# Transposes on TensorE that take two neighbouring bf16 values as one 32-bit word, in a fused convolution and gated-MLP kernel

## The chip, the cores and the metric

The kernel runs on one core of one Trainium2 chip. The metric is the device time of one execution in microseconds (us). The program is one instruction stream per engine: PE (TensorE, matmuls and transposes; PEld is its weight load), DVE (VectorE), ACT (ScalarE), POOL (GpSimd) and SP (which only issues DMAs here). Each engine works its stream in order, and semaphores hold it where it needs another engine's result.

## The reference, cut to what matters

The kernel computes a forward pass and all its gradients. With S = 2048 rows, D = 1024 and F = 3584:

```python
xn = layernorm(x)                       # S x D
g, u = xn @ w_gate, xn @ w_up           # S x F each
h = g * u
bm = h @ w_down                         # S x D
y = causal convolution of kv with the filter ssm_k, along S, by FFT   # per column
kv = shift_filter(k, shift_k) * v       # 4 taps
out = x + (xn * (y + kv * ssm_D)) * silu(bm)
grads of out for x, k, v, shift_k, ssm_k, ssm_D, w_gate, w_up, w_down
```

All inputs and outputs are bf16; the gradient of w_down needs h by rows, and the forward product needs h turned. A matmul contracts over the 128 partitions, so a matrix that lies by rows has to be turned before its columns can be contracted.

## The kernel before

The work is in stages, one after the other on PE, with other engines' work laid beside it.

**Stage 1, 0 to 52 us.** `layer_norm` (L554) normalizes 16 blocks of 128 rows in chunks of 1, 1, 2, 4, 4 and 4 blocks; most of this is DVE. The result of each block (128 rows by 1024 columns) is turned by eight PE transposes of 128x128 (L596 for the first two blocks, L607 and, for the last two chunks, L619 in `turn_late`) into a PSUM tile `tr`, and copied from there into `XNT` (one tile for four blocks, `[128, 8, 512]`: partition p, group dc, row s holds column dc*128+p). ACT copies even blocks (L609, L621), DVE odd ones (L611, L623): seven copies on DVE in all.

**Stage 2, up to 520 us.** `gu_unit` (L645) works on one slab of 256 columns of w_up and w_gate (14 slabs) and 4 blocks of rows at a time. For each block, 8 matmuls with 512 columns (L661; up and gate lie side by side) go into `psg`, which ACT copies to `gut` (L663). One unit later `multiply` (L672) lets DVE multiply the two halves into `hN` (L213, the line of the helper `tt`), POOL stores hN to DRAM as `Hd`, and a few groups later `turn` (L685) transposes hN on PE (L690, 8 for a unit of 4 blocks), ACT copies the PSUM tile to `hT` (L691), and SP stores that to DRAM as `HTd`, by rows of F. Weight slabs are loaded one slab ahead (`load_slab`, L536).

Beside it runs the forward convolution (`conv_forward`, L701): eight sub-steps `ds`, each an FFT of a piece of kv and one of filter rows, their product, and an inverse FFT. The large butterflies of the FFT are DVE operations at L213 and L283; the small DFTs are PE matmuls against tables (L235), which ACT copies to `SP` (L257, L295; two buffers) for DVE's `W<-SP`. `h_rows` (L738) turns filter rows with PE transposes (L747, L749: 8 for each half, of columns that lie 8 apart) and ACT scales them into `hx` (L750).

What sets the order: the convolution is a generator that `make_pump` (L465) advances. Each of its steps yields an estimate of its DVE time; after each group of 8 matmuls `tick` (L932) advances it until the estimates reach a share of their total that follows the number of groups done. `net` (L244) takes 0.95 of the PE time that the step has entered in `pe_us` off the estimate; `h_rows` enters 0.47 us (L744). A framework then orders each engine's instructions and places the semaphores; the convolution's DVE operations are kept in program order.

**Stage 3, 520 to 719 us.** bm = h @ w_down from HTd (L985), and the gate with its gradients on DVE (`gate`, L1203), which turns the last blocks of `dbm` with eight transposes each (L1238).

**Stages 4 to 6, to the end.** The gradients of w_gate and w_up (L1339, L1356), of w_down (L1434, whose stationary operand is h from `Hd`, loaded by `load_h`, L1371) and of x (L1486), with the backward convolution on DVE beside them.

A transpose is `nc.tensor.transpose(out, in_, ident)`: in_ is loaded as weights, and an identity matrix is the moving operand. `keep_busy` (L519) multiplies the identity with itself 58 and 10 times at the start, to no other end than a busy PE.

Of the kernel before, what the change touches and what calls it, by code (L numbers as in the profile page):

```python
# [19 lines left out]
def build_kernel(  # L20
# [87 lines left out]
    KFd = dram.tile([8, P, 16, 256], BF16, name="KFd")  # L108
    DYFd = dram.tile([8, P, 16, 256], BF16, name="DYFd")
    GUd = dram.tile([NSL, 2, P, 2, 8, SLW], BF16, name="GUd")  # L110
    Hd = dram.tile([NSL, P, 2, NB, P], BF16, name="Hd")
    HTd = [[dram.tile([n, S // 2], BF16, name=f"HTd{i}{n}") for n in (24 * P, 4 * P)] for i in range(2)]
    DGd = dram.tile([NSL, 2, S, SLW], BF16, name="DGd")


    const = ctx.enter_context(tc.tile_pool(name="const", bufs=1))
    ident = const.tile([P, P], BF16, name="ident")
    make_identity(nc, ident[:])
    mhpi = const.tile([P, 1], F32, name="mhpi")
    nc.vector.memset(mhpi[:], -np.pi / 2)  # L120
    negpi = const.tile([P, 1], F32, name="negpi")
# [64 lines left out]
    def turn_tables(psp):  # L186

        for j in range(2):
            for rq in range(2):
                ps = psp.tile([P, 4, 2, P], BF16, name="psY")  # L190
                for i in range(4):
                    for k in range(2):
                        nc.tensor.transpose(ps[:, i, k, :], T4[j][:, 4 * rq + i, k, :], ident[:])
                nc.scalar.copy(out=TI[:, j, 4 * rq:4 * rq + 4], in_=ps[:])
                yield


    def pr(t, i, j):
        if j > i:
            return t[:, i:j + 1:j - i, :]  # L200
        return t[:, i:(j - 1 if j > 0 else None):j - i, :]

    PIN = [False]

# [7 lines left out]
    def tt(o, a, b, op):  # L212
        pinned(V.tensor_tensor(o, a, b, op))  # L213
# [304 lines left out]

    def keep_busy(n):  # L519
        for i in range(n):  # L520
            mm = nc.tensor.matmul(busy[:, i % 4, :], ident[:], ident[:], start=True, stop=True)
        return mm

    keep_busy(58)
# [11 lines left out]
    def load_slab(sl, eng):  # L536
        w = fw.tile([P, DC, 2, SLW], BF16, name="wslab")
        fs = slice(sl * SLW, (sl + 1) * SLW)
        for a, wsrc in ((0, B_w_up), (1, B_w_gate)):
            last = eng.dma_start(out=w[:, :, a, :], in_=wsrc[:, fs].rearrange("(dc p) f -> p dc f", p=P))  # L540
        return w, last

    def ln_load(b0, n, x4):
# [6 lines left out]

    tr_ln, act_copy = [None], [None]
    turn_rows = []

    def layer_norm(b0, n, x4):  # L554
        def small(name, dt=F32):
# [27 lines left out]
        for i in range(n):  # L583
            b = b0 + i
            q, qi = divmod(b, 4)
            if n == 4 and i < 2:
                nc.scalar.activation(x4[:, i, :], x4[:, i, :], ACT.Identity, bias=mean_f[:, i:i + 1])
            else:
                V.tensor_scalar(x4[:, i, :], x4[:, i, :], mean_f[:, i:i + 1], None, op0=ADD)
            last = V.tensor_scalar(x4[:, i, :], x4[:, i, :], RSTD[:, b:b + 1], None, op0=MUL)  # L590
            if b < 2:
                for hh in range(2):
                    ps = ps_st.tile([P, 4, P], BF16, name="tr")
                    for dc in range(4):
                        d0 = (4 * hh + dc) * P
                        tr_ln[0] = nc.tensor.transpose(ps[:, dc, :], x4[:, i, d0:d0 + P], ident[:])  # L596
                    act_copy[0] = nc.scalar.copy(out=XNT[0][:, 4 * hh:4 * hh + 4, b * P:b * P + P], in_=ps[:])  # L597
                if b == 0:
                    with tc.issue_after(tr_ln[0].ins):
                        keep_busy(10)  # L600
                continue
            if b0 >= 8:
                turn_rows.append((x4[:, i, :], q, qi))
                continue
            ps = ps_st.tile([P, DC, P], BF16, name="tr")
            for dc in range(DC):
                tr_ln[0] = nc.tensor.transpose(ps[:, dc, :], x4[:, i, dc * P:(dc + 1) * P], ident[:])  # L607
            if i % 2 == 0:
                act_copy[0] = nc.scalar.copy(out=XNT[q][:, :, qi * P:(qi + 1) * P], in_=ps[:])  # L609
            else:  # L610
                V.tensor_copy(XNT[q][:, :, qi * P:(qi + 1) * P], ps[:])  # L611
        c, r0 = divmod(b0, 8)
        return last, root, st(xnn[:, c, r0:r0 + n, :], x4[:, 0:n, :])

    def turn_late():
        for i, (x, q, qi) in enumerate(turn_rows):
            ps = ps_st.tile([P, DC, P], BF16, name="tr")
            for dc in range(DC):
                tr_ln[0] = nc.tensor.transpose(ps[:, dc, :], x[:, dc * P:(dc + 1) * P], ident[:])  # L619
            if i % 2 == 0:  # L620
                act_copy[0] = nc.scalar.copy(out=XNT[q][:, :, qi * P:(qi + 1) * P], in_=ps[:])  # L621
            else:
                V.tensor_copy(XNT[q][:, :, qi * P:(qi + 1) * P], ps[:])  # L623
        turn_rows.clear()

    nop = lambda: None
# [18 lines left out]
    def gu_unit(sl, b0, n, w, tick):  # L645

        if n == 4:
            turn_of[0] += 1
            if turn_of[0] % 3 == 0 and sl < NSL - 2:
                gut = U[5][:, 2048:4096].rearrange("p (a i f) -> p a i f", a=2, i=4)  # L650
            else:
                gut = fg.tile([P, 2, 4, SLW], BF16, name="gut")
            hN = fg.tile([P, 2, 4, P], BF16, name="hN", bufs=3)
        else:
            gut = lnp.tile([P, 2, 2, SLW], BF16, name="gut_s", bufs=6)
            hN = lnp.tile([P, 2, 2, P], BF16, name="hN_s", bufs=6)
        for i in range(n):
            q, qi = divmod(b0 + i, 4)
            ps = ps_gu.tile([P, 512], F32, name="psg")
            for dc in range(DC):  # L660
                gu_mm[0] = nc.tensor.matmul(ps[:], XNT[q][:, dc, qi * P:(qi + 1) * P],  # L661
                                            w[:, dc].rearrange("p a f -> p (a f)"), start=(dc == 0), stop=(dc == DC - 1))
            nc.scalar.copy(out=gut[:, :, i], in_=ps[:].rearrange("p (a f) -> p a f", a=2))  # L663
            flush(5)
            if i == 0:
                turn_late()
            hn[0]()
            hn[0] = nop
            tick()
        sta(GUd[sl, b0 // 8][:, :, b0 % 8:b0 % 8 + n], gut[:, :, 0:n])  # L670

        def multiply():  # L672
            with tc.issue_after(last.ins) if b0 + n <= 4 and chunk[0] <= 2 else nullcontext():
                by_half = lambda t: t.rearrange("p i (a f) -> p a i f", a=2)
                tt(hN[:, :, 0:n], by_half(gut[:, 0, 0:n]), by_half(gut[:, 1, 0:n]), MUL)
            st(Hd[sl][:, :, b0:b0 + n, :], hN[:, :, 0:n])
            defer(turn)
        hn[0] = multiply

        def store(hT):  # L680
            fr, so = sl % 12 * SLW, b0 % 8 * P
            ld(HTd[b0 // 8][sl // 12][fr:fr + SLW, so:so + n * P].rearrange("(a f) s -> f a s", f=P),
               hT[:, :, 0:n].rearrange("f a i s -> f a (i s)"))

        def turn():  # L685
            hT = fg.tile([P, 2, 4, P], BF16, name="hT") if chunk[0] > 5 else lnp.tile([P, 2, 4, P], BF16, name="hT_s", bufs=5)
            ps = ps_tr.tile([P, 2, 4, P], BF16, name="tr")
            for a in range(2):
                for i in range(n):
                    nc.tensor.transpose(ps[:, a, i, :], hN[:, a, i, :], ident[:])  # L690
            nc.scalar.copy(out=hT[:, :, 0:n], in_=ps[:, :, 0:n])  # L691
            store(hT)

    h_out = []
# [6 lines left out]
    def conv_forward():  # L701
# [36 lines left out]
        def h_rows(ds, c):  # L738
# [2 lines left out]
            hrow = S_["h", ds]  # L741
            if c == 0:
                S_["hx"] = cf.tile([P, NB, P], BF16, name="hx")
            pe_us[0] += 0.47  # L744
            ps = ps_tr.tile([P, 8, P], BF16, name="tr")
            with tc.issue_after(tr_ln[0].ins):
                nc.tensor.transpose(ps[:, 0, :], hrow[:, c, :, 0], ident[:])  # L747
            for r in range(1, 8):
                nc.tensor.transpose(ps[:, r, :], hrow[:, c, :, r], ident[:])  # L749
            nc.scalar.activation(S_["hx"][:, 8 * c:8 * c + 8, :], ps[:], ACT.Copy, scale=WSC)  # L750
            if c == 1:
                h_out.append(ds)
                if ds + 1 < 8:
# [449 lines left out]
    def gate(b, ps):  # L1203
# [31 lines left out]
        def turn():  # L1235
            ps = ps_tr.tile([P, DC, P], BF16, name=tr_name[0])
            for dc in range(DC):
                nc.tensor.transpose(ps[:, dc, :], dbm[:, dc * P:(dc + 1) * P], ident[:])  # L1238
            nc.scalar.copy(out=DBMT[b // 4][:, :, (b % 4) * P:(b % 4 + 1) * P], in_=ps[:])
        if b >= 12:  # L1240
            defer(turn)
# [127 lines left out]
            next(others, None)  # L1369

    def load_h(sl):  # L1371
        h = u8(HSL[sl % 3], "p (a b f) -> p a b f", a=2, b=NB)
        ld(h, Hd[sl])
        hs[sl] = h

    for e in later:
# [172 lines left out]
    for g in range(1, 4):  # L1549
        for b in (4 * g, 4 * g + 2):  # L1550
            end = b == NB - 2
            pss = [ps_x.tile([P, D], F32, name="psx") for i in range(2)]
            for n in range(12 if end else 14):
# [3 lines left out]
                    DBM[n] = u8((7, 0, 1, 9)[n], a=4)  # L1557
                    ld(DBM[n], DBMd[512 * n:512 * n + 512, :].rearrange("(b u) d -> u b d", u=P))
                if end and n == 4:
                    h = u8(2, "p (a b f) -> p a b f", a=2, b=NB)  # L1560
                    ld(h, Hd[NSL - 1])
                if end and n == 8:
                    ln_loads(NB - 1)
                if g < 3:
# [83 lines left out]
```

## Time and profile before

| what | value |
|---|---|
| median of 3 runs | 1929.96 us |
| lowest and highest run | 1929.68, 1931.19 us |
| span of the profiled execution | 1929.5 us |
| PE busy | 1906.4 us (99%), 10843 matmul records |
| DVE busy | 1549.6 us (80%) |
| ACT busy | 638.4 us (33%) |
| POOL busy | 330.5 us (17%) |
| HBM read and written | 194.00 and 185.64 MB |
| transposes of hN, records (L690) | 448, 219 ns each |
| transposes of filter rows (L747, L749) | 128, 218 and 226 ns each |
| ACT copies hT<-tr of 128x1024 (L691) | 52, 1018 ns each |

How to read the page: busy time is a union of the instructions' spans. Matmuls are pipelined: one of 512 columns lasts 379 ns, but in a row they start closer together, so the spacing of starts and not the duration is what a matmul costs in a sequence. A line such as `L690 PE MATMUL tr<-ident,hN` is a group of instructions of one line of the kernel: engine, operation, written tile, read tiles; behind it stand the shape, the number, the busy time and the mean duration, then the idle time of the engine ahead of them and what ended it. L213 is a helper that many parts use, so one goes by the tile's name there. In the waits, `A <- B: t, n, m` says that A waited for B for t us in all, n times, at most m.

### The profile page before, as it was taken

To read this page: it belongs to the slowest core of one execution; us is meant where nothing else is said; L and a number is where in the kernel's file an instruction comes from. 1 tells how busy PE (TensorE), PEld (TensorE's weight loads), DVE (VectorE), ACT (ScalarE), POOL (GpSimd) and SP (SyncE) were. 2 spreads that over 40 slices of the span, in tenths; PEclk is the share of its full clock that TensorE was granted. 3 is DMA by queue.
4 is the path that set the end of the run, shared out by engine and by line. 5 is a ranking of instruction groups with operands and counts; after the bars stand their busy time and mean duration, and the time that the engine had idled before them with its cause. 6 is when DMAs were issued, how large, how long until landed. Compare 5 with 4: busy or idle time off the path is not lost.

```text
span 1929.5 us, 27354 instructions
## 1 busy us (share of the span) xinstructions
PE 1906.4 (99%) x10843; PEld 1031.0 (53%) x10978; DVE 1549.6 (80%) x1730; ACT 638.4 (33%) x942; POOL 330.5 (17%) x461
## 2 busy tenths in 40 slices
PE   8999999999999999999999999999999999999999
PEld 5555555555444456665666666664444444444444
DVE  9999999999937556888899999999996404288884
ACT  5764555555422233343222222222212102011113
POOL 4121212111112210000122131121211101011111
PEclk9999999999999999999999999999999999999999
DMA  8876866758899997666788788575787999889985
GB/s 293 268 259 217 261 209 226 234 196 268 272 270 311 282 313 258 208 202 219 258 246 261 239 248 262 202 272 174 226 253 174 157 205 210 153 170 201 191 177 169
DMA packets 451361, 444.43 MB, mean 230 GB/s; under 512 B 268801, under 2 KB 371613, under 8 KB 436769
## 3 DMA queue, kind: packets, MB, share of 16 engines
q1 hardware_dynamic: 394848, 243.36, 48.0%
q0 software_dynamic: 40064, 169.95, 27.8%
q10 hardware_dynamic: 16320, 29.36, 4.2%
q8 instruction: 86, 1.41, 0.3%
q14 instruction: 43, 0.34, 0.1%
HBM read 194.00 MB, written 185.64 MB: 197 GB/s over the span
## 4 chain that ended last, share of the span: by engine, by line
PE 71%; DVE 18%; DMA 4%; issue 4%; ACT 1%; SPq 1%; POOL 0%; DVEq 0%; ACTq 0%; POOLq 0%
PE psb L1356 20%; PE psb L1339 10%; PE psbm L985 10%; PE psx L1486 10%; PE psb L1434 9%; PE psg L661 6%; DVE W L213 4%; DVE KX L213 2%; DVE HX L213 2%; PE psF L235 2%; DVE dkp L1184 2%; DVE m L213 1%; DVE U L213 1%; DMA dkT<-DKSHd 1%; DVE hN L213 1%
## 5 line engine op out<-in xcount | busy, mean ns | idle before, releaser
L661 PE MATMUL psg<-wslab,U 128*128 128x512 bf16 x1733 | 401.6, 379 | 4.8 <-ACT U L597 1.0
L1356 PE MATMUL psb<-U,U 128*128 128x512 bf16 x1792 | 397.0, 379 | 0.0
L1486 PE MATMUL psx<-U,dgut 128*128 128x512 bf16 x1505 | 331.2, 379 | 2.4 <-DMA dgut<-DGd 0.8
L1486 PEld LDWEIGHTS <-dgut 128*128 128x128 bf16 x1792 | 175.2, 98 | 212.5 <-DMA dgut<-DGd 1.3
L1356 PEld LDWEIGHTS <-U 128*128 128x128 bf16 x1792 | 175.3, 98 | 197.9
L661 PEld LDWEIGHTS <-U 128*128 128x128 bf16 x1792 | 172.5, 98 | 187.3 <-issue 1.8
L1339 PE MATMUL psb<-wdt,U 128*128 128x256 bf16 x1792 | 205.6, 273 | 0.0
L1339 PEld LDWEIGHTS <-U 128*128 128x128 bf16 x1792 | 175.3, 98 | 29.2
L1434 PE MATMUL psb<-U,U 128*128 128x512 bf16 x797 | 175.9, 379 | 0.9
L213 DVE TENSOR_TENSOR W<-W 128x1024 f32<-128x1024 f32 (+1 forms) x174 | 171.6, 1003 | 3.7
L1361 ACT CAST wb<-psb 128x512 bf16<-128x512 f32 x112 | 65.6, 586 | 315.4 <-PE psb L1356 307.3
L985 PE MATMUL psbm<-U,ht 128*128 128x512 bf16 x658 | 144.8, 379 | 0.7
L1434 PEld LDWEIGHTS <-U 128*128 128x128 bf16 x896 | 87.5, 98 | 104.5
L663 ACT CAST gut<-psg 128x512 bf16<-128x512 f32 x156 | 91.6, 588 | 120.8 <-PE psg L661 118.9
L1518 ACT ACTIVATE dx_t<-dxn 128x1024 bf16<-128x1024 f32 x15 | 15.9, 1058 | 325.5 <-DVE dxn L213 325.5
L1184 DVE SCALAR_TENSOR_TENSOR dkp<-dkT,kT 128x1024 bf16<-128x1024 bf16 (+2 forms) x64 | 78.4, 1224 | 39.9 <-DMA dkT<-DKSHd 37.9
L985 PEld LDWEIGHTS <-ht 128*128 128x128 bf16 x672 | 65.7, 98 | 78.6
L213 DVE TENSOR_TENSOR U<-U,dht 128x2048 bf16<-128x2048 bf16 x56 | 68.3, 1221 | 46.4 <-ACT dht L1341 46.4
L1341 ACT CAST dht<-psb 128x512 bf16<-128x512 f32 x112 | 65.7, 587 | 116.3 <-PE psb L1339 116.3
L66 POOL DMA_DIRECT2D Hd<-hN x54 | 37.0, 685 | 292.9 <-DVE hN L213 291.8
L213 DVE TENSOR_TENSOR dxn<-psx,dxna_t 128x1024 f32<-128x1024 f32 x15 | 18.3, 1222 | 79.5 <-PE psx L1486 75.4
L1465 ACT CAST wbs<-psb 128x512 bf16<-128x512 f32 x51 | 29.9, 586 | 145.3 <-PE psb L1434 134.3
(260 smaller groups left out, 2464.6 us busy)
## 6 DMA issues: line engine op xcount, KB each, us to landing
U<-GUd SPq DMA_DIRECT2D x28, 1024.0 KB, 7.7
DGd<-U SPq DMA_DIRECT2D x28, 1024.0 KB, 6.0
GUd<-gut ACTq DMA_DIRECT2D x39, 512.0 KB, 6.0
out_dram<-wb SPq DMA_DIRECT2D x112, 128.0 KB, 3.9
U<-Hd SPq DMA_DIRECT2D x14, 1024.0 KB, 6.0
Hd<-hN POOLq DMA_DIRECT2D x54, 256.0 KB, 4.0
HTd<-hT SPq DMA_DIRECT2D x52, 256.0 KB, 3.9
ht<-HTd SPq DMA_DIRECT2D x6, 1536.0 KB, 11.4
```

The lines of the kernel that those rows point to most:

```text
L213: pinned(V.tensor_tensor(o, a, b, op))
L235: mm = nc.tensor.matmul(ps[:, k].rearrange("p (c d) -> p c d", c=2), T[:, r, k, :], xr[:, r], start=(n == 0), stop=(n == len(rs) - 1 and ( ...
L661: gu_mm[0] = nc.tensor.matmul(ps[:], XNT[q][:, dc, qi * P:(qi + 1) * P], w[:, dc].rearrange("p a f -> p (a f)"), start=(dc == 0), stop=(dc ...
L663: nc.scalar.copy(out=gut[:, :, i], in_=ps[:].rearrange("p (a f) -> p a f", a=2))
L985: mm = nc.tensor.matmul(ps[:, dh * 512:(dh + 1) * 512], ht(fc)[:, i * P:(i + 1) * P], WD[fc // 4][:, fc % 4, dh * 512:(dh + 1) * 512], sta ...
L1184: ins = V.scalar_tensor_tensor(prod[:].rearrange("p r d -> p (r d)")[:, lo:H], dkT[:, 0, lo:H], 1.0, kT[:, 0, 13 + m + lo:13 + m + H], op0 ...
L1339: nc.tensor.matmul(ps[:, x * SLW:(x + 1) * SLW], DBMT[2 * hf + g][:, dc, (b % 4) * P:(b % 4 + 1) * P], wdt[:, dc, :], start=(dc == 0), sto ...
L1341: nc.scalar.copy(out=dht[:, 2 * e:2 * e + 2].rearrange("p b f -> p (b f)"), in_=ps[:])
L1356: nc.tensor.matmul(ps[:], XN[b // 4][:, b % 4, dc * P:(dc + 1) * P], dgus[b // 8][:, :, b % 8], start=(b == 0), stop=(b == NB - 1))
L1361: nc.scalar.copy(out=wb[:, dc % 2].rearrange("p a f -> p (a f)"), in_=ps[:])
L1434: nc.tensor.matmul(ps, h[:, f, b, :], DBM[b // 4][:, b % 4, dh * 512:(dh + 1) * 512], start=(b == 0), stop=(b == NB - 1))
L1486: nc.tensor.matmul(ps[:, dh * 512:(dh + 1) * 512], t[n][:, f, i * P:(i + 1) * P], WGU[n][:, f, dh * 512:(dh + 1) * 512], start=(n == 0 and ...
```

## The change

Two neighbouring bf16 values are read as one 32-bit word, and PE turns words. A 128x128 transpose of words carries 256 columns, so there are half as many: 4 in place of 8. In PSUM, the two halves of a word lie beside each other; the copies out of PSUM read every second bf16 (`halves_of`) and so part the halves again.

A turned word holds two columns 2j and 2j+1 in one partition, so the order of the columns changes, and everything that is contracted with them follows:

- XNT: the words of a row are taken at steps of 4 words, so that partition p holds columns 8p to 8p+7. The weight slabs are loaded in the same order (`(p c) f` in place of `(dc p) f`).
- hN lies as rows of 256 columns in place of two halves of 128; Hd follows, and `load_h` views it so that the matmuls at L1434 find what they found. hT holds columns 2f and 2f+1 in partition f; the store to HTd puts them at rows 2f and 2f+1, so HTd is as it was.
- Filter rows: pairs of residues (2r, 2r+1) are one word; 4 transposes for each half, and `hx` is written as before. The entry in `pe_us` is 0.25.
- The identity is an f32 tile; the transposes that stay bf16 (the tables at L193, dbm at L1238) and `keep_busy` read the upper halves of its words as a bf16 identity with a step of 2.

Matmuls, DMAs and DVE operations stay the same in number, apart from that. The core of the diff:

```diff
-    Hd = dram.tile([NSL, P, 2, NB, P], BF16, name="Hd")
+    Hd = dram.tile([NSL, P, NB, SLW], BF16, name="Hd")
...
-    ident = const.tile([P, P], BF16, name="ident")
-    make_identity(nc, ident[:])
+    ident4 = const.tile([P, P], F32, name="ident4")
+    make_identity(nc, ident4[:])
+    ident = ident4[:].bitcast(BF16)[:, 1::2]
...
+    def turn_pairs(out, in_):
+        return nc.tensor.transpose(out, in_, ident4[:])
+
+    def halves_of(ps):
+        return ps.bitcast(BF16).rearrange("p q (s two) -> p q two s", two=2)
...
-            last = eng.dma_start(out=w[:, :, a, :], in_=wsrc[:, fs].rearrange("(dc p) f -> p dc f", p=P))
+            last = eng.dma_start(out=w[:, :, a, :], in_=wsrc[:, fs].rearrange("(p c) f -> p c f", c=DC))
...
+    def by_pair(t):
+        return t.rearrange("p (q two) s -> p q two s", two=2)
+
+    def in_pairs(x):
+        return x.bitcast(F32).rearrange("p (m q) -> p q m", q=4)
+
+    def turn_row(i, x, q, qi):
+        ps = ps_st.tile([P, 4, P], F32, name="tr")
+        for dc in range(4):
+            tr_ln[0] = turn_pairs(ps[:, dc, :], in_pairs(x)[:, dc])
+        to = by_pair(XNT[q][:, :, qi * P:(qi + 1) * P])
+        if i % 2 == 0:
+            act_copy[0] = nc.scalar.copy(out=to, in_=halves_of(ps[:]))
+        else:
+            V.tensor_copy(to, halves_of(ps[:]))
...
-            hN = fg.tile([P, 2, 4, P], BF16, name="hN", bufs=3)
+            hN = fg.tile([P, 4, SLW], BF16, name="hN", bufs=3)
...
-                by_half = lambda t: t.rearrange("p i (a f) -> p a i f", a=2)
-                tt(hN[:, :, 0:n], by_half(gut[:, 0, 0:n]), by_half(gut[:, 1, 0:n]), MUL)
-            st(Hd[sl][:, :, b0:b0 + n, :], hN[:, :, 0:n])
+                tt(hN[:, 0:n], gut[:, 0, 0:n], gut[:, 1, 0:n], MUL)
+            st(Hd[sl][:, b0:b0 + n, :], hN[:, 0:n])
...
-            ld(HTd[b0 // 8][sl // 12][fr:fr + SLW, so:so + n * P].rearrange("(a f) s -> f a s", f=P),
+            ld(HTd[b0 // 8][sl // 12][fr:fr + SLW, so:so + n * P].rearrange("(f a) s -> f a s", a=2),
...
-            ps = ps_tr.tile([P, 2, 4, P], BF16, name="tr")
-            for a in range(2):
-                for i in range(n):
-                    nc.tensor.transpose(ps[:, a, i, :], hN[:, a, i, :], ident[:])
-            nc.scalar.copy(out=hT[:, :, 0:n], in_=ps[:, :, 0:n])
+            ps = ps_tr.tile([P, 4, P], F32, name="tr")
+            for i in range(n):
+                turn_pairs(ps[:, i, :], hN[:, i, :].bitcast(F32))
+            nc.scalar.copy(out=hT[:, :, 0:n].rearrange("f a i s -> f i a s"), in_=halves_of(ps[:, 0:n]))
...
-            pe_us[0] += 0.47
-            ps = ps_tr.tile([P, 8, P], BF16, name="tr")
+            pe_us[0] += 0.25
+            ps = ps_tr.tile([P, 4, P], F32, name="tr")
+            pairs = hrow.rearrange("p c u r -> p (c u r)").bitcast(F32).rearrange("p (c u r) -> p c u r", c=2, r=4)
             with tc.issue_after(tr_ln[0].ins):
-                nc.tensor.transpose(ps[:, 0, :], hrow[:, c, :, 0], ident[:])
-            for r in range(1, 8):
-                nc.tensor.transpose(ps[:, r, :], hrow[:, c, :, r], ident[:])
-            nc.scalar.activation(S_["hx"][:, 8 * c:8 * c + 8, :], ps[:], ACT.Copy, scale=WSC)
+                turn_pairs(ps[:, 0, :], pairs[:, c, :, 0])
+            for r in range(1, 4):
+                turn_pairs(ps[:, r, :], pairs[:, c, :, r])
+            nc.scalar.activation(by_pair(S_["hx"][:, 8 * c:8 * c + 8, :]), halves_of(ps[:]), ACT.Copy, scale=WSC)
...
-        h = u8(HSL[sl % 3], "p (a b f) -> p a b f", a=2, b=NB)
-        ld(h, Hd[sl])
+        h = u8(HSL[sl % 3], "p (b a f) -> p a b f", a=2, b=NB)
+        ld(U[HSL[sl % 3]][:].rearrange("p (b f) -> p b f", b=NB), Hd[sl])
```

The first two blocks (L596) are turned in the same way, with two PSUM tiles of two words' transposes each; `turn_late` and the body of `layer_norm` call `turn_row`.

More of the change, by code (lines that the diff above doesn't have):

```diff
@@ L192, in turn_tables @@
                     for k in range(2):
-                        nc.tensor.transpose(ps[:, i, k, :], T4[j][:, 4 * rq + i, k, :], ident[:])
+                        nc.tensor.transpose(ps[:, i, k, :], T4[j][:, 4 * rq + i, k, :], ident)
                 nc.scalar.copy(out=TI[:, j, 4 * rq:4 * rq + 4], in_=ps[:])
@@ L520, in keep_busy @@
         for i in range(n):
-            mm = nc.tensor.matmul(busy[:, i % 4, :], ident[:], ident[:], start=True, stop=True)
+            mm = nc.tensor.matmul(busy[:, i % 4, :], ident, ident, start=True, stop=True)
         return mm
@@ L592, in layer_norm @@
                 for hh in range(2):
[L593 to L597, printed above, removed]
+                    ps = ps_st.tile([P, 2, P], F32, name="tr")
+                    for dc in range(2):
+                        tr_ln[0] = turn_pairs(ps[:, dc, :], in_pairs(x4[:, i, :])[:, 2 * hh + dc])
+                    act_copy[0] = nc.scalar.copy(out=by_pair(XNT[0][:, 4 * hh:4 * hh + 4, b * P:b * P + P]), in_=halves_of(ps[:]))
                 if b == 0:
@@ L604, in layer_norm @@
                 continue
[L605 to L611, printed above, removed]
+            turn_row(i, x4[:, i, :], q, qi)
         c, r0 = divmod(b0, 8)
@@ L616, in turn_late @@
         for i, (x, q, qi) in enumerate(turn_rows):
[L617 to L623, printed above, removed]
+            turn_row(i, x, q, qi)
         turn_rows.clear()
@@ L652, in gu_unit @@
                 gut = fg.tile([P, 2, 4, SLW], BF16, name="gut")
-            hN = fg.tile([P, 2, 4, P], BF16, name="hN", bufs=3)
+            hN = fg.tile([P, 4, SLW], BF16, name="hN", bufs=3)
         else:
             gut = lnp.tile([P, 2, 2, SLW], BF16, name="gut_s", bufs=6)
-            hN = lnp.tile([P, 2, 2, P], BF16, name="hN_s", bufs=6)
+            hN = lnp.tile([P, 2, SLW], BF16, name="hN_s", bufs=6)
         for i in range(n):
@@ L1237, in turn @@
             for dc in range(DC):
-                nc.tensor.transpose(ps[:, dc, :], dbm[:, dc * P:(dc + 1) * P], ident[:])
+                nc.tensor.transpose(ps[:, dc, :], dbm[:, dc * P:(dc + 1) * P], ident)
             nc.scalar.copy(out=DBMT[b // 4][:, :, (b % 4) * P:(b % 4 + 1) * P], in_=ps[:])
@@ L1559, in build_kernel @@
                 if end and n == 4:
-                    h = u8(2, "p (a b f) -> p a b f", a=2, b=NB)
-                    ld(h, Hd[NSL - 1])
+                    h = u8(2, "p (b a f) -> p a b f", a=2, b=NB)
+                    ld(U[2][:].rearrange("p (b f) -> p b f", b=NB), Hd[NSL - 1])
                 if end and n == 8:
```

## The prediction

> **What bounds the kernel now.** I read the page's totals and slices first, then the table by stages, the waits, and the timeline where PE last waits for DVE.
>
> ```profile
> PE 1906.4 (99%) x10843; PEld 1031.0 (53%) x10978; DVE 1549.6 (80%) x1730; ACT 638.4 (33%) x942; POOL 330.5 (17%) x461
> ...
> PE   8999999999999999999999999999999999999999
> ...
> DVE  9999999999937556888899999999996404288884
> ```
>
> PE looks like the bound everywhere. But up to slice 11 (530 us) DVE is full as well, and nearly all transposes that change lie there. The stages (columns: stretch, length, then the busy time of each engine):
>
> ```profile
> 10.00:52.00 42.00, 38.39 (x271) 20.63 (x274) 40.20 (x118) 27.00 (x44) 19.35 (x27) 1.00 0.91 303
> 52.00:492.00 440.00, 431.32 (x2666) 243.19 (x2715) 435.42 (x391) 256.88 (x358) 75.47 (x107) 1.00 0.72 238
> 492.00:520.00 28.00, 27.68 (x148) 13.77 (x152) 27.69 (x33) 12.30 (x20) 4.45 (x6) 1.00 0.85 287
> 520.00:560.00 40.00, 39.77 (x210) 20.09 (x212) 12.30 (x11) 9.79 (x12) 1.84 (x2) 1.00 0.80 225
> ```
>
> From 52 to 492 us DVE works 435.4 of 440 us and PE 431.3. DVE has 4.6 us left; it can't follow a PE that is 15 us quicker. Which waits for which shows in the waits of 52 to 530 us and in the timeline at 492 us:
>
> ```profile
> ACT SP L257 <- DVE W L213: 5.3, 5, 1.6
> PE psF L235 <- DVE kv L213: 3.4, 2, 1.9
> ...
> PE tr L690 <- DVE hN L213: 1.7, 1, 1.7
> ```
>
> ```profile
> 491.43 0.68 DVE L213 TENSOR_TENSOR hN<-gut 128x1024 bf16<-128x1024 bf16 x1
> 492.03 1.22 DVE L213 TENSOR_TENSOR W<-SP 128x1024 f32<-128x1024 f32 x1
> 492.16 0.45 PEld L690 LDWEIGHTS <-hN 128*128 128x128 bf16 x8 [2.20 <-DVE hN L213]
> 492.17 0.62 PE L690 MATMUL tr<-ident,hN 128*128 128x128 bf16 x8 [1.71 <-DVE hN L213]
> ```
>
> PE and ACT wait for DVE; no large wait of DVE for PE is listed. The last meeting is at 492.16: PE stands until DVE has multiplied that hN. From there PE's own work runs without a gap to the first L985 at 519.43: in the compiled order 116 matmuls of 512 columns, 24 transposes and 8 matmuls of 256, which at 216, 56 and 109 ns are 27.3 us, and 492.1 + 27.3 = 519.4. (Spacings come from groups of the timeline: ten L661 in 2.32 us with the last 0.379, so 1.94/9 = 216; eight L690 as below; 64 L1339 in 7.15 us, 109.) After 520 us DVE is 30% busy and PE nearly full, so a shift of 519.4 goes straight to the end. **The end is set by: DVE's work ahead of that multiply, plus PE's work behind it.**
>
> **The change part by part.** The rows of today:
>
> ```profile
> 146.01 0.61 PE L690 MATMUL tr<-ident,hN 128*128 128x128 bf16 x8
> ...
> 147.88 0.60 PE L749 MATMUL tr<-ident,U 128*128 128x128 bf16 x7
> ```
>
> ```profile
> L213 DVE TENSOR_TENSOR W<-SP 128x1024 f32<-128x1024 f32 x64 | 74.3, 1220 | 1.3 <-ACT yf L765 0.5
> L623 DVE COPY U<-tr 128x1024 bf16<-128x1024 bf16 x4 | 2.6, 680 | 0.0
> L611 DVE COPY U<-tr 128x1024 bf16<-128x1024 bf16 x3 | 2.0, 675 | 0.0
> ```
>
> *Transposes.* One lasts 219 ns, but in a row they follow every (610-219)/7 = 56 ns, and every (600-226)/6 = 62 where the weights are read at 16-byte steps (L749). Of 704 transposes (448 of h, 128 of normalized rows, 128 of filter rows) 352 remain. Today they are 576 x 56 + 128 x 62 = 40.2 us of PE. The trace has no 32-bit matmul. Bounds of one: 56 ns, as now; 109, as a matmul with as many bytes of moving data (256 columns of bf16); 216, if the array goes through the words four times (as 512 columns); 317, if load (98) and matmul (219) don't overlap. I take 62, since rows and filter words are now read at 16-byte steps like L749, and one instruction still moves 128 columns: PE work falls by 40.2 - 21.8 = 18 us, 15 of it from 52 to 492 us. All of that turns into waiting for DVE. Where does the price matter? From 60 to 520 us PE's nominal work is 451 us, 31 of it transposes (408 of h, 128 of filter rows); 268 remain, and 420 + 268 x price passes the 460 us plus 2 at **about 155 ns**.
>
> [...]
>
> *Copies out of PSUM.* They now read halves of words, 4 bytes apart. On ACT, 1024 f32 (L257, 1019 ns) and 1024 bf16 (L691, 1018 ns) cost the same, so nothing; were they to double, ACT would go from 257 to some 323 of 440 us and still be hidden. On DVE they don't cost the same: the seven copies of L611 and L623 take 680 ns for 1024 bf16, while an f32 read of 1024, also 4 bytes apart, takes 1220. Bounds 0 and 7 x 0.54; I take the upper, the row with the same spacing of data: **+3.7 us**, all between 18 and 52 us, where DVE is full, so paid at 492.
>
> [...]
>
> *The planner.* The filter rows' entry falls from 0.47 to 0.25, so convolution units count as longer and DVE gets them later in the program. Ahead of the multiply that ends at 492.11 the new DVE order has two W<-SP (1.135 us apart) and two KX steps (0.602) fewer: **-3.5 us**. PE's part behind it grows: 123 x 216 + 16 x 109 + 12 x 62 ns = 29.1 against 27.3: **+1.8 us**. The deferred units run after 520 us, where DVE is idle from 531 to 554 and PE's next use of them (L449) is at 542.9, 12 us late enough.
>
> *Layouts.* The hN multiply keeps its 1024 elements (684 ns). Hd's lines double to 2 KB; its stores stay 256 KB each and lie on POOL, busy 75 of 440 us. HTd stores keep their size and place on SP's queue. Weight slabs take rows 8p to 8p+7, still 512-byte pieces; a slab lands in 5.8 and 8.4 us and is wanted some 35 us later, so nothing; only the first has no cover (PE waits 0.6 us for it at 14.5). The f32 identity is made by POOL before the warm-up matmuls (1.4 to 7.5 us), which hide it; the 64 transposes that stay bf16 read it at 4-byte steps, by L749 against L690 at most 64 x 6 ns = 0.4 us, mostly hidden. A new wait: DVE's paired copies (rows 1 and 3) now stand together ahead of the next statistics and might wait for PE: 0 to 1 us; queued behind them is all of DVE. I take 0.
>
> *Sum:* +3.7 - 3.5 + 1.8 = +2.0 us. The profiled span is 1929.5 and the median 1929.96, 0.46 around it: 1931.5 + 0.46 = **1932.0**.
>
> **Rivals.**
> 1. *The word goes through in four passes* (the saving isn't there): 352 x 216 = 76 against 40.2, +35.8 us of PE. Decides from 155 ns. PE's present waits (8.5 us from 60 to 520, some 8 before) take up to 17: +19 to +36, say 27: **1957**. For it: 32-bit operands and no row of them. Against: one instruction per transpose in the compiled order, and it must carry bits unchanged. This is the other side, slower. 0.12.
> 2. *In between* (110 to 200 ns, or load and matmul overlapping badly): PE and DVE both late at their meetings, +4 to +11: **1937**. 0.13.
> 3. *PE's saving counts in full*: 1930 - 18 = **1912**. It needs DVE to have slack. 4.6 us of idle in 440 speaks against; for it, PE's 71% of the chain of waits. 0.08.
> 4. The forecast, DVE sets the end: without the DVE copies' loss 1928.3, with 1 us of waits and other DVE delays up to 1937. 0.67.
>
> **How the numbers follow.** A measurement of this kernel tells 0.2% (3.9 us) from no change. Of the forecast's 0.67, 0.48 lies within, 0.16 above, 0.03 below; of rival 2, 0.11 above and 0.02 within; rival 1 is slower, rival 3 faster. Faster 0.11, same 0.50, slower 0.39. The range leaves out rivals 1 and 3 (0.20): 1925 to 1943.
>
> **What would show it.** Right: word transposes about 62 ns apart; the seven DVE copies near 1.22 us; DVE still full from 10 to 531 us; PE with 15 us more of waits for DVE or for ACT behind DVE; the first psbm near 521.4. Wrong: spacings over 155 ns (rival 1); PE gaps unchanged and psbm near 502 (rival 3); DVE copies at 0.68 us (psbm near 517.7).

## The result

The changed kernel takes **1935.27 us** (median of 20 executions, 1933.50 to 1944.75), the kernel before 1930.48 in the same sitting (20 executions): ratio 1.0025, 95% interval 1.0017 to 1.0034. It is 4.8 us slower, just over what such a measurement can tell, where 1932.0 was forecast. By profiled spans, 1934.0 against 1929.5, it is 4.5 us.

The two stretches around the last meeting of PE and DVE, in the changed kernel (stretch, length, then the busy time of PE, weight loads, DVE, ACT and POOL, the granted TensorE clock, DMA share, GB/s):

```profile
52.00:492.00 440.00, 432.77 (x2451) 243.87 (x2451) 435.67 (x392) 258.23 (x359) 69.66 (x108) 1.00 0.72 239
492.00:520.00 28.00, 27.42 (x127) 13.47 (x128) 25.30 (x32) 11.59 (x19) 3.87 (x7) 0.89 0.67 228
```

Up to 492 us nothing is new: DVE is full (435.7 of 440), and PE is as busy as before (432.8 against 431.3), although it issues half as many transposes. The news stands in the second row: the clock was 0.89, not 1.00. The timeline of PE and DVE shows where:

```profile
487.53 1.24 PE L671 MATMUL psg<-wslab,U 128*128 128x512 bf16 x5
...
491.75 0.69 DVE L220 TENSOR_TENSOR hN<-gut 128x1024 bf16<-128x1024 bf16 x1
...
492.58 1.09 PE L205 MATMUL tr<-ident,hN 128*128 128x128 f32 x4 [3.81 <-DVE hN L220]
493.47 4.72 PE L671 MATMUL psg<-wslab,U 128*128 128x512 bf16 x11
```

The 56th hN multiply (the 50th of the full ones, with four blocks) ends at 492.44, 0.33 later than before. But PE has stood for 3.81 us by then, not 1.71, and the eleven matmuls of 512 columns behind its transposes take 4.72 us, where ten took 2.32 before. The short stretches give the reason (same columns):

```profile
486.00:490.00 4.00, 2.77 (x15) 1.35 (x13) 3.93 (x8) 1.65 (x3) 0.00 (x0) 1.00 0.64 154
490.00:492.00 2.00, 0.00 (x0) 0.00 (x0) 1.97 (x4) 0.00 (x0) 0.00 (x0) 0.76 0.81 256
...
494.00:496.00 2.00, 2.00 (x6) 0.63 (x5) 2.00 (x3) 1.30 (x2) 0.48 (x1) 0.50 1.10 415
...
498.00:500.00 2.00, 2.00 (x14) 1.26 (x13) 1.97 (x3) 1.09 (x3) 0.00 (x0) 1.00 0.89 238
```

The granted clock falls to half during the stand and comes back before 498; slices of half a microsecond put it at 0.50 from 491.06 to 497.89. PE's work from 492.58 on ran in it at half speed: 5.3 us, of which half, 2.7, is lost. The first psbm (the first matmul of bm, where stage 3 begins) starts at 524.84 instead of 519.43. Finally, the instructions that the change made, by groups (count, then min/median/max in ns, first and last start):

```profile
L205 PEld LDWEIGHTS tr<-ident,hN x216: 138/141/229, 50.6 to 530.3; 128*128 128x128 f32 x108
L205 PE MATMUL tr<-ident,hN x216: 272/273/446, 50.8 to 530.4; 128*128 128x128 f32 x108
L205 PEld LDWEIGHTS tr<-ident,U x112: 195/210/222, 27.7 to 440.8; 128*128 128x128 f32 x112
L205 PE MATMUL tr<-ident,U x112: 272/283/387, 27.7 to 440.9; 128*128 128x128 f32 x112
...
L575 DVE COPY U<-tr x7: 1201/1218/1220, 19.1 to 56.9; 128x1024 bf16<-128x1024 bf16 x7
```

and in a row, by the timeline:

```profile
145.97 0.65 PE L205 MATMUL tr<-ident,U 128*128 128x128 f32 x4
...
150.07 0.60 PE L205 MATMUL tr<-ident,hN 128*128 128x128 f32 x4
```

A word transpose of h follows the one ahead after (600 - 273)/3 = 109 ns, one whose words lie 16 bytes apart after (650 - 283)/3 = 122 (the trace's starts give a median of 120). So 224 x 109 + 128 x 120 ns = 39.8 us of PE, against 40.2 before: **half as many at about twice the price**.

### The profile page after: what moved, and what is told of

Same layout as the page of the kernel before. It is cut to its first block, busy times and chain, and to the rows that moved or that the text cites. A ratio compares the mean times of both kernels' runs of the same rounds, so it can differ in the third digit from the quotient of the medians.

```text
span 1934.0 us, 26795 instructions
## 1 busy us (share of the span) xinstructions
PE 1916.3 (99%) x10626; PEld 1033.6 (53%) x10626; DVE 1554.1 (80%) x1730; ACT 639.1 (33%) x942; POOL 320.6 (17%) x461
## 4 chain that ended last, share of the span: by engine, by line
PE 84%; DVE 12%; issue 2%; DMA 1%; ACT 1%; SPq 0%; POOL 0%; DVEq 0%; ACTq 0%
PE psb L1365 20%; PE psx L1495 20%; PE psb L1348 10%; PE psbm L994 10%; PE psb L1443 9%; PE psg L671 9%; DVE W L220 3%; DVE KX L220 2%; PE psF L242 2%; DVE HX L220 2%; DVE U L220 2%; PE psY L445 1%; DVE hN L220 1%; PE tr L205 1%; DVE m L220 1%
## 5 line engine op out<-in xcount | busy, mean ns | idle before, releaser
L671 PE MATMUL psg<-wslab,U 128*128 128x512 bf16 x1792 | 409.7, 380 | 2.9 <-DMA wslab<-in_B_w_gate_dram 0.8
L66 POOL DMA_DIRECT2D Hd<-hN x54 | 29.5, 547 | 294.1 <-DVE hN L220 285.6
```

## The experiments

**Theory.** DVE sets the end up to its 56th hN multiply, so the 0.54 us more of each DVE copy are paid; the planner's new number gives about as much back; then PE's longer stand at that multiply lets the clock fall, and PE's work behind it takes longer. A word's price costs nothing. **Rival A:** the words' price (109 to 120 ns) makes the loss. **Rival B:** the planner's new order makes it. Later a **rival C:** the low clock is a by-product. Each kernel was timed beside the kernel before on the same chip; that one took 1930.71, 1931.05 and 1930.42 us in the three sittings (kernels 1 to 4, 5 to 8, 9 to 12). All times below are medians; the other columns are of the profiled execution alone.

| kernel | multiply ends | PE stands | first psbm | time | ratio, 95% interval |
|---|---|---|---|---|---|
| before | 492.11 | 1.71 | 519.43 | 1930.48 | |
| changed | 492.44 | 3.81 | 524.84 | 1935.27 | 1.0025, 1.0017-1.0034 |
| 1 rows as bf16 | 488.36 | 3.8 | 519.84 | 1931.16 | 1.0003, 0.9995-1.0012 |
| 2 changed, planner 0.47 | 496.36 | 0.6 | 523.76 | 1935.06 | 1.0023, 1.0014-1.0032 |
| 3 before, planner 0.25 | 488.02 | 3.71 | 520.54 | 1931.01 | 1.0000, 0.9991-1.0009 |
| 4 changed, copies on ACT | 491.39 | 3.8 | 522.85 | 1933.71 | 1.0018, 1.0009-1.0026 |
| 5 changed, stand filled | 493.03 | - | 522.77 | 1936.26 | 1.0020, 1.0004-1.0036 |
| 6 changed, late turn | 492.74 | - | 518.54 | 1931.15 | 1.0003, 0.9989-1.0018 |
| 7 before, 0.25, late turn | 488.99 | - | 514.83 | 1927.27 | 0.9978, 0.9970-0.9987 |
| 8 changed, words twice | - | - | - | 1962.47 | 1.0169, 1.0149-1.0190 |
| 9 as 5 | 493.11 | - | 522.85 | 1933.89 | 1.0031, 1.0018-1.0045 |
| 10 before, copies twice | 497.05 | 1.7 | 524.36 | 1934.88 | 1.0026, 1.0015-1.0037 |
| 11 before, late turn | 493.19 | - | 519.12 | 1929.79 | 0.9995, 0.9986-1.0003 |
| 12 as 7, words for h and filter | 487.57 | - | 513.36 | 1926.89 | 0.9980, 0.9972-0.9989 |

**1. Rows turned as bf16 again** (slabs and DVE copies as before, the other words kept).

```diff
...
-        for dc in range(4):
-            tr_ln[0] = turn_pairs(ps[:, dc, :], in_pairs(x)[:, dc])
...
+        for dc in range(DC):
+            tr_ln[0] = nc.tensor.transpose(ps[:, dc, :], x[:, dc * P:(dc + 1) * P], ident)
...
```

> The changed kernel with the normalized rows turned as bf16 again (their 128 transposes, their copies and the weight slabs' layout as before); words for h and the filter rows stay, and so does the planner's 0.25. Theory (DVE sets the end, and a wait of PE for DVE at 490 us costs clock): the seven DVE copies go from 1218 to 680 ns, the 56th hN multiply ends 3.8 us earlier, at 488.6 instead of 492.44, PE hardly waits there (under 1 us instead of 3.8), its granted clock stays 1.0 from 491 to 498, the first psbm comes 4.5 to 6 us earlier than 524.84: 1929 to 1930.5 us. Rival A (the price of a word transpose, 109 to 120 ns, makes the loss): only 64 words of 480 go, so at most 0.5 us comes back: 1934.5 to 1935.5. Rival B (the planner's new order makes it): no change, 1934.5 to 1935.5.

1931.16 us, 0.7 over the expected range. The multiply ends 4.08 us earlier and the first psbm 5.0, so the loss goes with the rows, as the theory had it; rivals A and B, which expected 1934.5 and more, fall for the bulk. The details of the theory failed, though: PE still stands 3.8 us (not under 1), because it is ready for the meeting 4.1 us earlier too (484.68 instead of 488.77). The clock also still falls, but for 3.4 us in this profile, not 6.8 (same columns):

```profile
486.00:490.00 4.00, 1.50 (x6) 1.01 (x7) 3.93 (x7) 0.51 (x1) 0.68 (x2) 0.83 0.94 313
490.00:492.00 2.00, 2.00 (x6) 0.73 (x5) 2.00 (x3) 1.09 (x2) 0.40 (x1) 0.50 1.11 421
492.00:494.00 2.00, 2.00 (x13) 1.08 (x11) 2.00 (x2) 0.78 (x2) 0.00 (x0) 0.98 0.97 390
```

**2. The changed kernel with the planner's old number**, and **3. the kernel before with the new one** (the edit of kernel 2; that of kernel 3 is its reverse):

```diff
-            pe_us[0] += 0.25
+            pe_us[0] += 0.47
```

> The changed kernel with one number put back: the planner's entry for filter rows is 0.47 again. Theory: DVE's copies still cost 3.8, and the two W<-SP and two KX stand ahead of the 56th hN multiply again (+3.5), so it ends near 496; PE waits about 7 us there, the granted clock drops as in the changed kernel (2.5 to 3 us), PE's work behind is 27.3 instead of 29.1: first psbm near 526.3, some 1.5 us later than in the changed kernel: 1936 to 1937.5 us. Rival B (the new order makes the loss): 1930 to 1931. Rival A (price of words): no change, 1935.

> The kernel before with the planner's entry for filter rows at 0.25 instead of 0.47, and nothing else. Theory: the 56th hN multiply ends near 488.6; PE comes there at 490.5 and doesn't wait, and has 29.1 us behind it: first psbm near 519.5, 1929.5 to 1930.5 us, no drop of the clock at 491 us. Rival B (the new order makes the loss): 1933 to 1935.

2: 1935.06, below the expected 1936 to 1937.5. The multiply stands at 496.36, as expected. But PE stands only 0.6 us there and the clock stays at 1.00. So a late multiply doesn't make the long stand. 3: 1931.01, 0.5 over the expected range: nothing lost or won, against rival B. And without a single word in it, it has the long stand and the slow matmuls:

```profile
483.13 1.24 PE L661 MATMUL psg<-wslab,U 128*128 128x512 bf16 x5
488.08 1.04 PE L690 MATMUL tr<-ident,hN 128*128 128x128 bf16 x8 [3.71 <-DVE hN L213]
488.91 4.90 PE L661 MATMUL psg<-wslab,U 128*128 128x512 bf16 x11
```

The planner's number makes the stand: kernel 3 has it with the new number (3.71 us), kernel 2 hasn't with the old one. It moves 1.8 us of PE's work from ahead of the meeting to behind it (the prediction's own 29.1 against 27.3; kernel 3's trace has the 123 matmuls of 512 columns and the 16 of 256 of that sum). The hN multiply ends 4.1 us earlier, while PE is ready for it 6.1 us earlier (484.37 instead of 490.46): by this working 4.1 because earlier meetings tie PE to DVE, which isn't shown meeting by meeting, and 1.8 for the moved work. So PE would stand 1.7 + 1.8 = 3.5 us; 3.7 to 3.8 are measured. The expectation that no clock falls here failed with it. In kernel 3 the fall isn't in every execution: the four with a mean clock of 1.0 took 1928.2 to 1929.3 us, the seven with 0.997 to 0.999 took 1930.4 to 1933.8.

Kernels 1 and 3 together answer rival A: they differ only in the words for h and the filter rows and the layouts that go with these, 1931.16 and 1931.01.

**4. The seven copies on ACT.**

```diff
-        if i % 2 == 0:
-            act_copy[0] = nc.scalar.copy(out=to, in_=halves_of(ps[:]))
-        else:
-            V.tensor_copy(to, halves_of(ps[:]))
+        act_copy[0] = nc.scalar.copy(out=to, in_=halves_of(ps[:]))
```

> The changed kernel with the seven copies of row transposes that stand on DVE (1218 ns each) put on ACT. Theory: DVE has 8.5 us less ahead of the 56th hN multiply, PE doesn't wait there, the clock stays 1.0, first psbm 517.5 to 519.5: 1927.5 to 1930.5 us, unless DVE then waits for ACT between 18 and 52 us (ACT is busy 27 of 42 us there, so 7 more fit). Rival A (price of words): 1934.5 to 1935.5, since all words stay. Rival B (planner): 1934.5 to 1935.5.

1933.71: 1.6 us below the changed kernel, of the 8.5 that DVE is spared; the theory missed by 3 us. New waits of DVE took most of the gain (the first two lines lie from 10 to 56 us, the third from 56 to 130; total, times, longest):

```profile
DVE hN L220 <- ACT gut L670: 2.3, 2, 2.0
DVE rr L593 <- ACT r__579 L589: 1.1, 1, 1.1
...
DVE W L220 <- ACT SP L302: 2.8, 1, 2.8
```

From 10 to 52 us ACT has room as a sum (29.7 of 42 busy), but DVE waits for single results that now stand behind copies in ACT's queue. From 56 to 130 us PE is full (73.7 of 74) and DVE waits there, by way of ACT: relieved of so much, it is busy 70.3 us of 74 where it was 73.2 in the changed kernel. A stand of 2.02 us at 31.8 us was also followed by a clock of 0.50 for 3.4 us; what each of these made of the loss isn't shown.

**5 and 9. The stand filled**: 32 idle word transposes, which nothing reads.

```diff
...
             ps = ps_tr.tile([P, 4, P], F32, name="tr")
+            nth[0] += n == 4
+            if nth[0] == 50 and n == 4:
+                for i in range(32):
+                    turn_pairs(ps[:, i % 4, :], ident4[:])
```

> The changed kernel with 32 idle word transposes of the identity (3.5 us at 109 ns; nothing reads them) put on PE ahead of the transposes of the 56th hN, where PE stood 3.8 us. No instruction of use is moved. Theory (the stand of 3.8 us makes the granted clock fall to 0.50 for 6 us, which costs 3 us): clock 1.0 from 488 to 500 us, the hN multiply still ends near 492.4, the first psbm comes at 521.5 to 522 instead of 524.84: 1931.5 to 1932.8 us. Rival C (the doubled matmul spacing behind the stand is contention for SBUF or late ACT reads, and the low clock a by-product): no gain, 1935 to 1935.5.

> The same kernel as in the fill experiment (32 idle word transposes in PE's stand of 3.8 us), run again: there the stage behaved as the theory said (clock 1.0, first psbm 522.77 instead of 524.84, 29.7 us behind the multiply instead of 32.4), but six of nine executions were 1.5 to 10 us longer than the other three, and the profiled one lost 4.4 us near 1664 us, where PE waited 2.5 us for a transfer. Theory: most executions at 1932.5 to 1933.5 us, some 2 below the changed kernel. Rival (the idle words cost as much as they save): median at 1935 or over with few low ones.

In both profiles the stage does what the theory says (timeline of the first):

```profile
489.44 3.71 PE L205 MATMUL tr<-ident 128*128 128x128 f32 x32
493.09 0.66 PE L205 MATMUL tr<-ident,hN 128*128 128x128 f32 x4
493.58 2.54 PE L673 MATMUL psg<-wslab,U 128*128 128x512 bf16 x11
```

Eleven matmuls take 2.54 us instead of 4.72, though the same multiply ends 0.6 us later; from its end to the first psbm pass 29.74 us in both, against 32.40 in the changed kernel: 2.7 us are the clock's, against rival C. The whole times say less. The first sitting was scattered (1932.7 to 1942.6, a 2.5-us wait for a transfer at 1662 in its profile); its median of 1936.26 lies over the expected range and decides nothing; in the second, 1933.89, seven of ten executions took 1933.1 to 1934.5 (the interval of its ratio overlaps that of the changed kernel). That is 1.4 below 1935.27, not 2.7, and over the expected 1933.5; by the ratios (1.0031 and 1.0025), in which the three long executions weigh, no gain shows. So the 2.7 us are shown for the stage, not for the whole time. Profiles show why they need not be the same: with the same stand of 3.82 us the clock was low for only 3.4 us in kernels 1 and 4, and there 31.5 us pass from the multiply to the first psbm, 1.7 over 29.74. The changed kernel has executions with a mean clock of 1.0 (two of twenty, 1933.5 and 1934.0), with 0.999 (nine, 1934.3 to 1935.4) and with 0.998 (seven, among them the profiled one, 1935.4 to 1936.6). That these are falls of none, 3.4 and 6.8 us is argued from the mean clocks, not shown.

**6 and 7. The turn put later**: the transposes of that hN three units later in PE's order, in the changed kernel and in kernel 3.

```diff
...
-            defer(turn)
+            nth[0] += n == 4
+            later.append([-3 if nth[0] == 50 and n == 4 else 0, turn])
```

> The changed kernel with the transposes of the 56th hN put three units (some 14 us) later in PE's order; the multiply stays where it is. Theory: PE no longer stands 3.8 us at 488.6, the clock stays 1.0, and PE's 29.1 us of work end near 518 instead of 524.84 (at worst PE meets DVE again a little later and gets half of it): 1927.5 to 1931 us. Rival C (only the stand counts, not the clock): first psbm 521, 1931 to 1932. If DVE's work ahead, not PE's, sets what follows: no change, 1935.

> The kernel before with the planner's entry at 0.25 and the same turn put three units later; no words anywhere. Theory: DVE's lead of 4.1 us that the entry gives (seen with the entry alone: multiply at 488.02 instead of 492.11) was lost to a stand of 3.7 us and a low clock; without them the first psbm comes near 514 to 517 instead of 520.54: 1924.5 to 1928.5 us, faster than both kernels. Rival: PE meets DVE elsewhere and nothing is won, 1930 to 1931.

1931.15 and 1927.27. The stand is gone, the clock is 1.00, and the first psbm comes 6.3 and 5.7 us earlier. The time of kernel 6 lies between the theory's range and rival C's; its psbm of 518.54, where the rival had 521, speaks for the theory. Kernel 7 keeps DVE's lead of the planner's number up to the first psbm, by its timeline (the last line from a longer stretch of it):

```profile
484.10 3.62 PE L663 MATMUL psg<-wslab,U 128*128 128x512 bf16 x16
...
497.51 0.61 PE L693 MATMUL tr<-ident,hN 128*128 128x128 bf16 x8
...
514.83 1.46 PE L988 MATMUL psbm<-U,U 128*128 128x512 bf16 x6
...
521.62 0.62 PE L693 MATMUL tr<-ident,hN 128*128 128x128 bf16 x8 [1.65 <-DVE hN L213]
```

Behind the first psbm PE meets DVE again: it stands 1.65 us for a later hN, and 1.81 in kernel 6 (at 525.48). So both profiled spans are 4.1 us shorter, less than the psbm's lead. Kernel 7 is faster than both kernels, by 3.8 us against the one before beside it.

**8. Each word transpose issued twice**, with the same result.

```diff
+        nc.tensor.transpose(out, in_, ident4[:])
         return nc.tensor.transpose(out, in_, ident4[:])
```

> The changed kernel with each of its 352 word transposes issued twice (same operands, same result), so that one costs about 225 ns: the price of the rival of four passes. Theory: PE's nominal work from 60 to 520 us rises to 420 + 268 x 0.225 = 480 us, past the 460 that DVE leaves, and PE gets late by some 15 to 18 us there and 3 to 6 before: 1950 to 1959 us, PE's waits gone, DVE waiting for ACT and PE. If every PE microsecond counted: 352 x 0.112 = 39 us, 1974. If PE's words never counted up to this price: 1935 to 1937.

1962.47, 27.2 over the changed kernel: 3.5 over the expected range, and well below the 39 of all its PE work. So a crossing point lies between the two prices: at the present one the words cost next to nothing, at this one most of their time. In the profile PE takes the bound over and DVE waits behind it (the stage, then DVE's two largest waits from 10 to 530 us; this execution was 11 us longer than the other four, so its lines show the kind of wait, not the sum):

```profile
52.00:492.00 440.00, 436.96 (x2546) 261.54 (x2593) 412.69 (x362) 248.24 (x338) 67.58 (x104) 1.00 0.67 221
```

```profile
DVE hN L221 <- ACT gut L674: 11.6, 13, 1.8
DVE W L221 <- ACT SP L265: 6.4, 3, 3.2
```

**10. DVE's copies twice in the kernel before**: the suspected cost by itself, without words or layouts.

```diff
                 V.tensor_copy(XNT[q][:, :, qi * P:(qi + 1) * P], ps[:])
+                V.tensor_copy(XNT[q][:, :, qi * P:(qi + 1) * P], ps[:])
```

> The kernel before with each of DVE's seven copies of row transposes out of PSUM done twice (same source, same target), and nothing else: 7 x 0.6 to 0.68 = 4.2 to 4.8 us more on DVE, no words, no new layout, the planner's 0.47. Theory (DVE's work ahead of the 56th hN multiply goes to the end in full): multiply and first psbm 4.2 to 5.2 us later, PE's stand at the meeting not longer than in before, clock 1.0: 1934.3 to 1935.8 us, as the changed kernel with the old planner's number (1935.06). Rival (the words' price or the layouts made that loss): 1930 to 1931.5.

1934.88, as expected. Seven more copies of 0.68 us, 4.8 us, put the multiply 4.94 and the first psbm 4.93 later, and PE's wait is to the tenth that of before:

```profile
PE tr L692 <- DVE hN L213: 1.7, 1, 1.7
```

DVE's work ahead of the meeting goes to the end one for one. The clock is 1.00 at the meeting; earlier in this profile, behind a stand of 1.75 us at 53 us, it was 0.50 for 3.4 us; the multiply still came only 0.2 us later than the copies explain.

**11. The late turn in the kernel before alone.**

> The kernel before with the transposes of the 56th hN three units later and nothing else (the planner's 0.47). Theory: PE's stand there was 1.7 us (2.2 with the weight load) and had no low clock behind it, so at most that is won: first psbm 517.2 to 517.9 instead of 519.43: 1928 to 1929.3 us. With the planner's 0.25 the same move won 3.7. Rival (the late turn by itself wins the 3.7): 1926.5 to 1927.5.

1929.79, 0.5 over the expected range and within what can be told from no change. Behind the multiply 25.9 us are left instead of 27.3, so 1.4 of the 1.7 are won there, but in this profile DVE reached the multiply 1.1 us later, a difference it already had at its first convolution step (54.80 against 53.74). The large gain needs the planner's number as well.

**12. Kernel 7 with words for h and the filter rows** (kernel 1 with the late turn).

> Words for h and the filter rows, rows as bf16, the planner's 0.25, and the late turn: the fastest kernel so far plus 288 words instead of 576 bf16 transposes. In that kernel PE, not DVE, runs without a gap from 484 to 515 us, so a word's price must show. Theory: 224 words at 109 ns for 448 at 56, and 64 at 120 for 128 at 62, are 32.1 us against 33.0: no change within 0.2% of 1927.3 us, 1926 to 1928.5. If a word cost 62 ns: 14 us less PE work, and at least part of it seen: under 1925. If words hinder in another way (weight loads that don't overlap): over 1930.

1926.89, as expected, ratio 0.9980 against 0.9978 of kernel 7; from the multiply to the first psbm pass 25.8 us in both. Where PE itself sets the pace, 288 words do neither better nor worse than 576 bf16 transposes. This and kernel 7 are the fastest versions; what wins is the late turn with the planner's number, not the words.

## Why the prediction was right and wrong

The mechanism was right in the main: the end is DVE's work ahead of the 56th hN multiply plus PE's work behind it. Of the signs that the prediction named, the DVE copies near 1.22 us and the full DVE came true; words 62 ns apart, 15 us more of PE's waits and a first psbm near 521.4 (it came at 524.84) did not. Its terms, by the profiles:

- **"Word transposes about 62 ns apart"**: wrong, 109 and 120. I chose the row by columns and by the step of the weights; the bound I passed over, "a matmul with as many bytes of moving data", had the figure. (Its weight load took 141 and 210 ns.) The 18 us of PE that were to turn into waiting did not exist: PE is as busy as before. Since both prices lie under the crossing point of 155 ns, the end hardly moved: 12 words lie behind the multiply, 12 x (109 - 62) = **0.6 us**.
- **"+3.7 us" for the DVE copies**: right in size (1218 ns for 1220 forecast, 675 and 680 before, 7 x 0.54), and paid at the meeting. With all else of the words it came to 4.25 (kernel 2 against before) and 4.08 (changed against kernel 1). So 0.3 to **0.5** us are left beside the copies; whether they are the "0 to 1 us" of waits that I took as 0 isn't shown.
- **"-3.5 us" of the planner ahead of the multiply**: 4.1 (kernel 3) and 3.9 (changed against 2), right with a little to spare. **"+1.8 us behind it"**: with the 0.6 above, 27.3 + 2.4 = 29.7, and the filled kernels show 29.74.
- **What was missing**: PE's stand at the meeting. I worked out that 1.8 us of PE's work move behind the multiply, and did not ask what PE does in the time ahead of it: it stands, 3.8 instead of 1.7 us. The clock falls (0.50 for 6.8 us), and the 29.7 us take 32.4: **2.7 us** in the profiled execution, 1.7 where the fall lasts 3.4 us (kernels 1 and 4).

Together in the profiles: multiply +0.33, work behind it +2.4, clock +2.7, which is the +5.4 of the first psbm; behind that the changed kernel is 0.9 quicker (1409.2 against 1410.1 us to the end), giving 4.5. Forecast were +0.2 and +1.8. By the medians it is simpler: the planner's number wins and loses nothing (kernel 2 against the changed kernel, kernel 3 against the one before), since what DVE gains by it goes into PE's later work, the stand and the clock. What is left of the change is the DVE copies: 4.1 us come back without the words of the rows (kernel 1), and 4.5 us are lost by twice the copies alone (kernel 10).

At the meeting, the stands of 3.71 and 3.81 us (kernel 3, the changed one) had a clock of 0.50 behind them, and that of 1.71 (before) left it at 1.00; that the length decides isn't shown, since three shorter stands elsewhere were followed by 0.50 as well (the last section). The profile of before, at 1.00 in every stretch of 20 us up to 1920, had no fall to learn this from. No table of mine had the stand of the changed kernel, which 1.7 + 1.8 would have given.

The rivals: four passes (1) are not there (109 and 120 ns, not 216), and kernel 8 shows what about such a price costs (31.4 us over the kernel before, 27.2 over the changed one; the prediction said 19 to 36). Rival 2 had nearly the right price but not the mechanism: at the meeting PE waits for DVE, and longer than before. Rival 3's saving never came about. Layouts, ACT's copies (hT 1017 ns) and the identity cost nothing that shows.

## What to carry to other kernels

Here the price of a transpose went with the bytes it moves, not with its columns (109 and 120 ns for 128 columns of words, 56 and 62 for 128 of bf16, 109 for a matmul of 256 of bf16): where two values are packed into one word, look for the matmul row with as many bytes. When a change moves work of one engine to the far side of a meeting, work out how long that engine then stands ahead of it, and what the clock in the traces did behind such a stand (here 0.50 behind 3.7 to 3.8 us, 1.00 behind 1.7 at the same meeting). In this balanced pair of engines each extra microsecond of the slower one was paid in full (kernel 10: 4.8 us of copies, the first psbm 4.93 later), and taking just these off again gave them back (kernel 1: 4.1 us). Taking off twice as much by putting it on a third engine gave back 1.6 of 8.5 us (kernel 4), as new waits came up.

## What the runs showed of the hardware that was not expected

- A 128x128 transpose of 32-bit words starts every 109 ns, as a bf16 matmul of 256 columns does, its weight load takes 141 ns (bf16: 98) and 210 with words 16 bytes apart, where the spacing is 120. Whether the load or the moving words set the 109 ns isn't shown.
- After the stand of 3.7 to 3.8 us the granted clock was 0.50 in all four profiles that have it: for 6.8 us in the changed kernel and kernel 3, beginning 2.3 and 2.6 us after PE's last matmul, and for 3.4 us in kernels 1 and 4, beginning 0.2 and 1.3 us after PE had gone on. After 1.7 us at the same meeting (before, kernel 10) it did not fall. But shorter stands elsewhere were also followed by 0.50 for 3.4 us, beginning 0.2 to 1.5 us after PE had gone on: 1.75 us (kernel 10, at 53 us), 2.02 us (kernel 4, at 32 us) and 2.54 us (kernel 5, from 1662 us), while others of 1.5 to 1.9 us were not (before, at 298 and 412 us). So in these traces the length of a stand alone does not tell whether the clock falls.
